# A planned projection stage and a two-engine copy of the attention sums in a transformer block

## The chip, the cores and the metric

The kernel runs on one core of one Trainium2 chip. The metric is the device time of one execution in microseconds (us); the kernel before takes 2050.27 us in the median of three runs (2050.03 to 2050.84). PE is TensorE, DVE is VectorE, ACT is ScalarE, POOL is GpSimd, SP is SyncE, which here only issues DMA transfers.

## The reference

One pre-norm transformer block for 2048 tokens of width 640: 32 heads of 20 channels, and a gated feed-forward part of width 1728. Everything is f32.

```python
def _A_ref(x, wqkv, wo):
    qkv = (lambda x, *d: x.transpose(*d))((x @ wqkv).reshape(B, S, 3, H, Dh), 2, 0, 3, 1, 4)
    q, k, v = qkv[0], qkv[1], qkv[2]
    scores = jnp.einsum("bhqd,bhkd->bhqk", q, k) * (Dh ** -0.5)
    p = _softmax(scores, axis=-1)
    o = jnp.einsum("bhqk,bhkd->bhqd", p, v)
    return (lambda x, *d: x.transpose(*d))(o, 0, 2, 1, 3).reshape(B, S, D) @ wo
def _B_ref(x, w_gate, w_up, w_down):
    return (_silu(x @ w_gate) * (x @ w_up)) @ w_down
h = x + _A_ref(_layernorm(x, axis=-1), A_wqkv, A_wo)
h2 = h + _B_ref(_layernorm(h, axis=-1), B_w_gate, B_w_up, B_w_down)
```

## The kernel before, in words

**Precision.** A factor of a product is split into a rounded part `hi` and a remainder `lo`; ACT writes `hi`, and DVE or POOL subtracts it from the original to make `lo` (function `split`, L88 for `hi`, L89 for `lo`). A product is the sum of three terms, hi·hi, lo·hi and hi·lo.

**Start-up and projections (0 to 338.5 us).** The tokens are four chunks of 512. For each chunk the rows of `x` are loaded, normalized on DVE (statistics L124/L125, then one over the square root by three Newton steps of four small operations each, L98, then the scaling L703), turned round by PE transposes (L735 for the first chunk, L722 for the others, function `flip`), and split into `z_hi` and `z_lo`. The first two blocks of queries and keys run on the whole array (L760). All others are 64-row halves: each `step` of `query_key` or `value` gives PE two products (L547), one for each half of the array, and the two halves run beside each other. While this goes on, PE also computes first scores, whose row maxima the softmax needs later: for those, pairs of products go into one-bank tiles `ps_single` (L186, function `max_differences`, read by ACT L197 and DVE L199; and L210, `max_twice`, read by ACT L222 and DVE L216).

Queries, keys and values travel through DRAM: a finished block goes from PSUM to `e`, `q_stk` or `v_stk` in SBUF, from there to `qk_d` (SP, L305, `emit_store`), and back in the stacked layout that the attention wants (SP, L153, `stack`). SP issues in its program order. The stacked keys of early scores get a difference computed by POOL (L417).

The order of all this is decided when the program is built, by the class `Halves` (an object named `pe`). It keeps a clock for each half of the array and a time at which each engine is free; `pe.use(engine, us)` books work, `pe.sp` books the issue of transfers, `pe.pair` places a pair of score products where the model says that the operands have landed (`there`) and that a bank is free, `pe.flip` places transposes. The list `work` holds 72 items (blocks and value parts); at fixed items it splits weights (`split_w`), loads a chunk, starts a norm (`norm`) and turns the chunk round.

Constants are written by POOL: `k_stk` rows (L142), 14 tiles `mx` with a lowest value (L821), and two tiles `ev` of ones (L895). Three products L826 on `xt` keep PE busy while the first norm runs.

**Attention (338.9 to 1478 us).** 32 units of 16 key tiles. For each key tile PE makes four score products (L1300), ACT the exponential of each (L1306), and PE weighs the values with them (L1310) into one accumulator bank `acc`, of which there is one. In between, three score products per key tile go to `ps_max` (L229, three banks), whose maxima DVE takes (L235). A string for each key tile sets the order on PE: s and S are score products, m and M products for maxima, W the weighing of the key tile two back.

```python
ORDER = ("sMsSmSmW", "SmMsMsSW", "mSmMsSsW")
```

After the last key tile of a unit, `row_sums` copies `acc` to SBUF (L1320, ACT), and four transfers take the sums out of it (L1323).

**After attention (1480 to 2044 us).** Output projection, second norm (`moments` calls its Newton operations in groups), feed-forward part.

Of the kernel before, what the change touches and what calls it, by code (L numbers as in the profile page):

```python
# [47 lines left out]
def tile_block(ctx: ExitStack, tc: tile.TileContext, x, wqkv, wo, wg, wu, wd, out):  # L48
# [42 lines left out]
    def rstd_steps(pool, var, n, tag):  # L91
# [5 lines left out]
        def some(f, *args, **kw):  # L97
# [8 lines left out]
        ]  # L106
        better = [
            some(tt, out=t, in0=r, in1=r, op=ALU.mult),
            some(tt, out=t, in0=t, in1=v, op=ALU.mult),
            some(ts, t, t, -0.5, 1.5, op0=ALU.mult, op1=ALU.add),  # L110
            some(tt, out=r, in0=r, in1=t, op=ALU.mult),
# [189 lines left out]
    def emit():  # L301

        job = stores.pop(0)
        for dst, src, what in job["pieces"]:
            nc.sync.dma_start(dst, src)  # L305
            pe.sp(job["ready"])
            for which, n in what:
                landed[which] += n
                landing[which] = pe.free["sync"] + 3.0
        e_free[job["of"]] = pe.free["sync"] + 3.5  # L310
# [18 lines left out]
    with tc.tile_pool(name="pa", bufs=2) as pa:  # L329
# [10 lines left out]
        def split_sbuf(src, hi, lo, copy):  # L340

            nc.scalar.activation(copy, src, AF.Copy)
            split(copy, hi, lo, nc.gpsimd)
# [6 lines left out]
        def back(now=True):  # L350
            while coming and (not now or coming[0][0] <= pe.now()):
                assert all(landed[1, 0, c] == GD for c in range(NC))
                load_keys(0, coming.pop(0)[1])
                pe.sp(n=4)
# [11 lines left out]
        def place(t):  # L366
# [4 lines left out]
            pe.sp(n=2)  # L371
# [13 lines left out]
        def load_items():  # L385
            for lane, places in lanes:
                while lane:
# [12 lines left out]
                    pe.sp(n=4)  # L400
                    items[lane.pop(0)][3:5] = t, pe.free["sync"]
            for item in items:
                which, _, _, t, at, known, _, base = item
                if not which or t is None or known is not None or pe.now() < at + 4.0:
                    continue
# [10 lines left out]
                for b, a in differences:  # L416
# [3 lines left out]
                    item[5] = pe.use("pool", 1.3) + 0.2  # L420

        def there(n):
# [3 lines left out]
            return t is not None and pe.now() >= at + 4.5  # L426
# [3 lines left out]
        def staged_keys(u, kc, ks, q=None, since=0):  # L430
# [32 lines left out]
            if u == 0:  # L463
                first_unit[0] += len(all_products)
            return [
                (lambda: slot[0] >= since and all(map(there, ns)), lambda a=a: one(*a), a[2])
# [3 lines left out]
        early, others = [], []  # L470
# [37 lines left out]

        class Halves:
# [5 lines left out]
            def __init__(self):  # L515
                self.t = [0.0, 0.0]
                self.free = dict.fromkeys(("vector", "scalar", "pool", "sync"), 0.0)
# [17 lines left out]
            def sp(self, after=0.0, n=1):  # L535
                self.use("sync", 0.4 * n, after)
# [70 lines left out]
            def flip(self):  # L607
# [6 lines left out]
                self.use("pool", 1.3, self.free["scalar"] + 0.1)  # L614
                del self.single[0]

# [80 lines left out]
        def norm(c):  # L697
# [4 lines left out]
            def apply(t):  # L702
# [6 lines left out]
                [(1.1, lambda t=t: stats(pa, xs[c * TPC + t], mv[:, t, :])) for t in range(TPC)]  # L709
                + [(0.2, lambda f=f, g=g: (f(), g())) for f, g in zip(steps[::2], steps[1::2])]  # L710
                + [(0.6, lambda t=t: apply(t)) for t in range(TPC)]
# [7 lines left out]
        def flip(c, k):  # L719
# [6 lines left out]
            pe.flip()  # L726
            copy = chunks[c][:, :, k * P : (k + 1) * P]
            ps, z_hi, z_lo = (a.rearrange("p (t n) -> p t n", t=TPC) for a in (ps, z_hi, z_lo))
            split_sbuf(ps, z_hi, z_lo, copy)
# [37 lines left out]
        def keep(c, m, ps):  # L767
# [7 lines left out]
            else:  # L775
                free = pe.use("scalar", 0.5, start)
                done = pe.use("scalar", 0.5)
                ready = pe.use("pool", 1.3, done + 0.2)
                split_sbuf(ps, e[:, 0], e[:, 1], e[:, 1].bitcast(F32))
# [39 lines left out]
        for u in range(NU):  # L819
            if any(moved(u, kc) for kc in (1, 2)):  # L820
                nc.gpsimd.memset(mxs[u], LEAST)  # L821
        for i in range(4):
            load_w(i)
        warm = ps_one()
        for _ in range(3):
            nc.tensor.matmul(warm, ident, xs[TPC - 1][:, :CH], start=True, stop=True)  # L826
        new_z(0)
        for _, f in norm(0):
# [33 lines left out]
        lns, flips = [], []  # L862
        finish_at = len(work)
        for at, (kind, c, *which) in enumerate(work):
            slot[0] = at
            if at < 9:
                for i in range(split_at[at], split_at[at + 1]):
                    split_w(i + 2)
                    if i % 2 == 1 and loaded < 8:
                        load_w(loaded)  # L870
                        loaded += 1
# [6 lines left out]
            for n in range(1, NC):  # L878
                if at == (2 if n == 1 else begins(n) - 15):
                    lns = norm(n)  # L880
                if n > 1 and at == begins(n) - 16:
                    assert not flips
                    load_x(n)
            if kind == "first":
# [3 lines left out]
            for n in range(1, NC):  # L888
                if at == (7 if n == 1 else begins(n) - 3):
                    assert not lns and all(job["c"] == n - 1 for job in pe.jobs)  # L890
                    new_z(n)
                    flips = [(n, k) for k in range(ND)]
            if at == 6:
                for ev in evs:
                    nc.gpsimd.memset(ev, 1.0)  # L895
                pe.use("pool", 1.5)
# [1116 lines left out]
```

## Time and profile before

| what | us |
|---|---|
| median of 3 runs | 2050.27 (2050.03 to 2050.84) |
| the execution that was profiled | 2046.24 |
| its span in the profile | 2044.5 |
| PE busy in the span | 2012.1 (98%) |
| DVE busy | 1624.6 (79%) |
| ACT busy | 1462.0 (72%) |
| POOL busy | 766.6 (37%) |

The profiled execution is 1.74 us longer than its span and 4.03 us shorter than the median. A line of the profile names the source line, the engine, the operation, the tile written and the tile read; a bracket holds the idle time of the engine just before and what ended it. Matmuls overlap by design: five of them in 1.32 us do not take 0.26 us each, but one step apart plus the end of the last. PEld is the loading of weights into the array.

### The profile page before, as it was taken

How to read it: one execution, taken by the hardware profiler on the slowest of the kernel's cores; microseconds unless marked ns; L12 is line 12 of the kernel's file. 1: busy time of each engine (PE TensorE's matmuls, PEld its weight loads, DVE VectorE, ACT ScalarE, POOL GpSimd, SP SyncE). 2: the span in 40 equal slices, each digit the busy share in tenths (PEclk: the TensorE clock that was granted, in tenths of full speed). 3: DMA queues.
4: the chain of work that ended last, by engine and by line, in shares of the span. 5: the costliest groups of instructions: out<-in, count | busy, mean ns of one | idle time of the engine just before them, and what ended most of it. 6: DMA issues, size and time to landing. Idle time of an engine off the chain costs nothing.

```text
span 2044.5 us, 38964 instructions
## 1 busy us (share of the span) xinstructions
PE 2012.1 (98%) x13656; PEld 1234.4 (60%) x13656; DVE 1624.6 (79%) x3267; ACT 1462.0 (72%) x2937; POOL 766.6 (37%) x1074
## 2 busy tenths in 40 slices
PE   7999999999999999999999999999999999999999
PEld 5888887333333333333333333345598888888888
DVE  7778677888888888888888888886378666676677
ACT  3787888999999999999999999996724222211221
POOL 4443441434343434244431011001145454754555
PEclk9999999999999999999999999999999999999999
DMA  7766554243433443443433013211158654974542
GB/s 230 219 203 222 171 168 146 90 135 117 145 129 107 143 126 128 137 156 127 160 116 118 30 58 86 83 55 61 29 175 301 225 198 157 337 277 157 203 151 93
DMA packets 205123, 305.03 MB, mean 149 GB/s; under 512 B 47664, under 2 KB 82480, under 8 KB 203904
## 3 DMA queue, kind: packets, MB, share of 16 engines
q1 hardware_dynamic: 204832, 302.53, 45.4%
q8 instruction: 109, 1.79, 0.4%
q14 instruction: 86, 0.70, 0.1%
q10 hardware_dynamic: 96, 0.00, 0.0%
HBM read 205.78 MB, written 95.68 MB: 147 GB/s over the span
## 4 chain that ended last, share of the span: by engine, by line
PE 91%; DMA 3%; DVE 2%; POOL 1%; issue 1%; ACT 1%; SPq 0%; POOLq 0%; DVEq 0%; ACTq 0%
PE acc L1310 25%; PE ps_one L1300 16%; PE ps_a L1478 15%; PE ps_max L229 12%; PE ps_b L1572 8%; PE ps_one L547 8%; PE ps_single L210 2%; PE ps_max L1034 2%; PE ps_b L1034 1%; PE ps_single L186 1%; DMA k_stk<-qk_d 1%; DMA units<-w_d 1%; PE ps_one L760 0%; DVE mx L235 0%; PE ps_single L722 0%
## 5 line engine op out<-in xcount | busy, mean ns | idle before, releaser
L1306 ACT ACTIVATE probs<-ps_one 128x512 f32<-128x512 f32 x2048 | 1056.9, 616 | 60.1 <-PE ps_one L1300 23.8
L235 DVE TENSOR_REDUCE mx<-ps_max 128x1 f32<-128x512 f32 x1472 | 925.1, 684 | 117.2 <-PE ps_max L229 72.5
L1300 PE MATMUL ps_one<-q_stk,k_stk 62*128 62x512 f32 x2048 | 582.0, 430 | 0.6 <-ACT ev L807 0.6
L1310 PE MATMUL acc<-probs,v_stk 128*32 128x512 f32 x4096 | 545.2, 604 | 0.0
L229 PE MATMUL ps_max<-k_stk,q_stk 60*128 60x512 f32 x1472 | 488.6, 439 | 1.0 <-DVE mx L235 0.3
L1300 PEld LDWEIGHTS ps_one<-q_stk,k_stk 62*128 62x128 f32 x2048 | 289.4, 184 | 284.8 <-ACT probs L1306 270.8
L229 PEld LDWEIGHTS ps_max<-k_stk,q_stk 60*128 60x128 f32 x1472 | 244.6, 184 | 165.7 <-DVE mx L235 129.0
L1693 DVE TENSOR_TENSOR tmp<-ps_a,tmp 128x512 f32<-128x512 f32 x208 | 141.2, 689 | 120.3 <-PE ps_a L1478 93.5
L1310 PEld LDWEIGHTS acc<-probs,v_stk 128*32 128x32 f32 x4096 | 80.6, 108 | 181.0 <-issue 169.7
L1572 PE MATMUL ps_b<-halves,yp 128*128 128x320 f32 x1032 | 179.3, 308 | 1.7 <-POOL yp L89 1.2
L1572 PEld LDWEIGHTS ps_b<-halves,yp 128*128 128x128 f32 x1032 | 165.1, 188 | 18.2 <-POOL yp L89 1.5
L1478 PE MATMUL ps_a<-t,units 128*128 128x512 f32 x624 | 162.5, 396 | 0.0
L246 POOL CAST both<-neg 128x16 fp32r<-128x16 f32 x32 | 6.6, 206 | 367.7 <-PE ps_one L1300 147.5
L1478 PE MATMUL ps_a<-z,units 128*128 128x512 f32 x516 | 133.8, 394 | 0.0
L89 POOL TENSOR_TENSOR yp<-y,yp 128x256 fp32r<-128x256 f32 x96 | 60.2, 627 | 187.7 <-ACT yp L88 187.7
L1478 PEld LDWEIGHTS ps_a<-t,units 128*128 128x128 f32 x624 | 112.6, 188 | 18.6
L216 DVE CUSTOM_DVE_ANT_0 q_stk<-ps_single,q_stk 128x512 f32<-128x512 f32 x138 | 93.0, 689 | 31.4 <-ACT q_stk L222 25.1
L1577 DVE TENSOR_TENSOR h<-ps_b,h 128x320 f32<-128x320 f32 x248 | 110.0, 481 | 6.8 <-PE ps_b L1572 5.4
L1478 PEld LDWEIGHTS ps_a<-z,units 128*128 128x128 f32 x516 | 93.1, 187 | 15.9
L1345 POOL TENSOR_TENSOR o<-o,rb 128x512 f32<-128x512 f32 x31 | 39.8, 1284 | 159.8 <-DMA rb<-r_d 64.8
L88 ACT ACTIVATE yp<-tmp 128x512 fp32r<-128x512 f32 x40 | 25.3, 633 | 103.1 <-POOL tmp L1565 103.1
L547 PE MATMUL ps_one<-z_hi,w_lo 64*128 64x512 f32 x380 | 98.8, 397 | 0.0
(220 smaller groups left out, 3003.9 us busy)
## 6 DMA issues: line engine op xcount, KB each, us to landing
units<-w_d SPq DMA_DIRECT2D x186, 256.0 KB
w_d<-stage SPq DMA_DIRECT2D x106, 256.0 KB
halves<-j_d SPq DMA_DIRECT2D x70, 320.0 KB
k_stk<-qk_d SPq DMA_DIRECT2D x112, 160.0 KB
j_d<-stage SPq DMA_DIRECT2D x42, 320.0 KB
q_stk<-qk_d SPq DMA_DIRECT2D x64, 160.0 KB
k_stk<-qk_d SPq DMA_DIRECT2D x112, 80.0 KB
rb<-r_d SPq DMA_DIRECT2D x32, 256.0 KB
```

The source lines that it names most:

```text
L216: nc.vector.tensor_tensor_reduce(out=place, in0=pss[1], in1=place, scale=1.0, scalar=LEAST, op0=ALU.add, op1=ALU.max, accum_out=mx[:, b, p ...
L229: nc.tensor.matmul(ps, queries[u][rows, pair, t * P : (t + 1) * P], keys[u // NC][rows, pair, kc * CH : (kc + 1) * CH], start=True, stop=True,
L235: nc.vector.tensor_reduce(mxs[u][:, b, pair, t, kc : kc + 1], ps, axis=AX.X, op=ALU.max)
L547: product = nc.tensor.matmul(job["ps"][:, :out], lhs, rhs, start=(half == 0 and i == 0), stop=(half == 1 and i == job["n"] - 1),)
L1034: nc.tensor.matmul(ps[:, :HALF], a[:, k, :], w[:, k, hs], start=(n == 0), stop=(n == 3 * ND - 1),)
L1300: nc.tensor.matmul(ps, keys[u // NC][rows, p, kt * P : (kt + 1) * P], queries[u][rows, p, :], start=True, stop=True,)
L1306: nc.scalar.activation(probs[p][:, b, :], ps, AF.Exp, scale=scale)
L1310: nc.tensor.matmul(acc[32 * j : 32 * j + 32, :], values[u // NC][:, kt, j * VW : j * VW + 32], probs[j // 2][:, j % 2, :], start=(kt == 0) ...
L1478: nc.tensor.matmul(ps.rearrange("p (t n) -> p t n", t=TPC), w[k][:, i], z[k][:, :, j], start=(first and m == 0), stop=(last and m == len(n ...
L1572: nc.tensor.matmul(ps, a, b, start=(n == 0), stop=(n == len(pairs) - 1))
L1577: nc.vector.tensor_tensor(out=h, in0=ps, in1=h, op=ALU.add)
L1693: add = lambda out, ps, x: nc.vector.tensor_tensor(out=out, in0=ps, in1=x, op=ALU.add)
```

## The change

1. **The planner's model.** `pe.sp` now takes the bytes of a transfer and counts them at 330 KB/us in a clock of their own; it returns the time of landing, and the conditions for placing a pair (`there`, `landing`, the new `queries_at`) use that time in place of fixed allowances. The booking of L417 grows from 1.3 + 0.2 to 1.35 + 1.2, of a pair of Newton operations from 0.2 to 0.4, of a scaling from 0.6 to 1.2. Norm steps wait in the plan for the chunk to land (`x_at`), transposes for the norm (`normed`), and what is left is flushed at `begins(n) + 1`.
2. **Second parts on either engine.** `second_part` puts the subtraction that makes `lo` on DVE (0.75 in the model) when POOL would end over 1.0 later, else on POOL (1.3). Seven subtractions of `z_lo`, `e`, `v_stk` and `z_hi` move to DVE.
3. **Order of the terms** in `query_key`: hi·hi, then z_hi·w_lo, then z_lo·w_hi.
4. **Constants.** The `mx` and `ev` tiles are written by `fill_rest` at item 1 of `work`.
5. **Newton step** in three operations in place of four (12 become 9 for a norm).
6. `row_sums`: ACT copies columns 0 to 255 of `acc` (L1343), DVE columns 256 to 511 (L1344).
7. The products that keep PE busy at the start use a `ps_wide` tile; `moments` takes six Newton operations at a time.

```diff
-            some(tt, out=t, in0=r, in1=r, op=ALU.mult),
-            some(tt, out=t, in0=t, in1=v, op=ALU.mult),
-            some(ts, t, t, -0.5, 1.5, op0=ALU.mult, op1=ALU.add),
-            some(tt, out=r, in0=r, in1=t, op=ALU.mult),
+            some(stt, out=t, in0=r, scalar=-0.5, in1=v, op0=ALU.mult, op1=ALU.mult),
+            some(tt, out=t, in0=t, in1=r, op=ALU.mult),
+            some(stt, out=r, in0=t, scalar=1.5, in1=r, op0=ALU.add, op1=ALU.mult),
...
-            def sp(self, after=0.0, n=1):
-                self.use("sync", 0.4 * n, after)
+            def sp(self, after=0.0, n=1, kb=0):
+                end = self.use("sync", 0.4 * n, after)
+                begin = max(self.free["dma"], end - 0.4 * n + 0.5)
+                self.free["dma"] = begin + kb / 330
+                self.free["sync"] = max(end, self.free["dma"] - 5.0)
+                return max(self.free["sync"] + 2.0, self.free["dma"] + 1.3)
...
-            return t is not None and pe.now() >= at + 4.5
+            return t is not None and pe.now() >= at + 0.3
...
+            def second_part(self, after):
+                ends = [max(self.free[e], after, self.now()) + us for e, us in SECOND]
+                if ends[1] + 1.0 < ends[0] and self.free["vector"] < after + 0.5:
+                    return nc.vector, self.use("vector", SECOND[1][1], after)
+                return nc.gpsimd, self.use("pool", SECOND[0][1], after)
...
-            terms = ((z_hi, w_hi), (z_lo, w_hi), (z_hi, w_lo))
+            terms = ((z_hi, w_hi), (z_hi, w_lo), (z_lo, w_hi))
...
-        for u in range(NU):
-            if any(moved(u, kc) for kc in (1, 2)):
-                nc.gpsimd.memset(mxs[u], LEAST)
+
+        def fill_rest():
+            for ev in evs:
+                nc.gpsimd.memset(ev, 1.0)
+            for u in range(NU):
+                if any(moved(u, kc) for kc in (1, 2)):
+                    nc.gpsimd.memset(mxs[u], LEAST)
+            pe.use("pool", 3.5)
...
+                if at == n == 1:
+                    fill_rest()
...
-        nc.scalar.activation(o, acc, AF.Copy)
+        nc.scalar.activation(o[:, : CH // 2], acc[:, : CH // 2], AF.Copy)
+        nc.vector.tensor_copy(o[:, CH // 2 :], acc[:, CH // 2 :])
```

What it does to the order on the engines, at three places. The first is POOL in the first 35 us, with the change (w_lo is the lower part of a slice of the weights; the tiles' numbers are the buffers').

```order
L142 MEMSET k_stk_115 32x4096 x2
L89 TENSOR_TENSOR w_lo<-raw,w_hi 128x5x128 x2
L837 MEMSET ev_155 128x768
L837 MEMSET ev_156 128x768
L840 MEMSET mx_120 128x64
L840 MEMSET mx_121 128x64
L840 MEMSET mx_122 128x64
```

Eleven more `mx` tiles follow, and then three more `w_lo`. Before, the 14 `mx` tiles stood ahead of the first `w_lo`, and the two `ev` tiles behind the fifth; now all 16 stand between the second and the third `w_lo`.

The second place is SP's queue where the first pair of score products gets its queries, before (-) against after (+ and unmarked); `qk_d` is the DRAM buffer, `k_stk` and `q_stk` are stacked keys and queries.

```order
 L305 DMA qk_d<-q_stk 80x2x512
 L305 DMA qk_d<-q_stk 16x2x512
+L153 DMA k_stk_115<-qk_d 40x2x512
+L153 DMA k_stk_115<-qk_d 20x2x512
+L153 DMA k_stk_115<-qk_d 40x2x512
+L153 DMA k_stk_115<-qk_d 20x2x512
 L153 DMA q_stk<-qk_d 40x2x512
 L153 DMA q_stk<-qk_d 20x2x512
```

Four loads of keys now stand ahead of the four loads of those queries; before, they came behind them.

The third place is DVE at the end of an attention unit, with the change and with the semaphores that each instruction waits for (L235 takes a maximum, L1355 is the reciprocal of the sums, L242 ends a unit's maxima).

```order
L235 TENSOR_REDUCE mx_125<-ps_max 128x1 [waits PE_49] x6
L1344 COPY o<-acc 128x256 [waits DMAHW5_49,DMAHW4_49,DMAHW6_49,DMAHW3_49,Activation_49]
L235 TENSOR_REDUCE mx_125<-ps_max 128x1 [waits PE_49] x9
L1355 RECIPROCAL r<-r 128x16 [waits DMAHW3_49,DMAHW2_49,DMAHW4_49,DMAHW1_49,DMAHW0_49]
L235 TENSOR_REDUCE mx_125<-ps_max 128x1 [waits PE_49] x17
```

The copy L1344 is new among the maxima, and it waits for ACT's semaphore: the value it waits for is the one that ACT's own copy L1343 of the same unit sets. On PE the number of products and, from the attention on, their order are the same in both programs.

More of the change, by code (lines that the diff above doesn't have):

```diff
@@ L465, in staged_keys @@
             return [
-                (lambda: slot[0] >= since and all(map(there, ns)), lambda a=a: one(*a), a[2])
+                (
+                    lambda: slot[0] >= since and all(map(there, ns))
+                    and (q is not None or pe.now() >= queries_at.get(u, math.inf)),
+                    lambda a=a: one(*a), a[2],
+                )
                 for a in all_products
             ]
-        early, others = [], []
+        early, others, queries_at = [], [], {}
         def third_unit():
@@ L777, in keep @@
                 done = pe.use("scalar", 0.5)
[L778 to L779 removed]
+                engine, ready = pe.second_part(done + 0.2)
+                split_sbuf(ps, e[:, 0], e[:, 1], e[:, 1].bitcast(F32), engine)
             r0 = m // 2 * P
```

69 lines of the change are left out of this document (35 added, 34 removed).

## The prediction

> **What bounds the kernel now.** I read first the table of stretches, cut where PE's idle time or clock changes (columns: length, busy us of PE, PEld, DVE, ACT, POOL, granted clock, DMA share, GB/s).
>
> ```profile
> 26.40:46.00 19.60, 17.77 (x133) 14.96 (x132) 17.80 (x39) 8.36 (x13) 10.28 (x8) 1.00 0.66 207
> 46.00:48.00 2.00, 0.80 (x4) 0.54 (x6) 1.91 (x3) 0.38 (x1) 1.22 (x1) 1.00 0.61 166
> 48.00:52.00 4.00, 4.00 (x24) 3.77 (x22) 1.81 (x7) 1.77 (x5) 0.00 (x0) 0.57 0.82 245
> 52.00:100.00 48.00, 46.92 (x423) 41.37 (x421) 35.09 (x172) 38.00 (x104) 21.04 (x16) 1.00 0.72 219
> 100.00:220.00 120.00, 116.81 (x1076) 105.19 (x1073) 97.44 (x334) 97.35 (x202) 48.97 (x38) 1.00 0.66 209
> 236.00:239.00 3.00, 0.69 (x8) 0.37 (x6) 1.40 (x4) 0.82 (x2) 2.58 (x3) 1.00 0.59 203
> 239.00:243.00 4.00, 4.00 (x29) 3.85 (x27) 1.60 (x5) 1.79 (x3) 0.00 (x0) 0.57 0.00 0
> 243.00:338.50 95.50, 93.61 (x925) 87.77 (x923) 73.96 (x253) 78.34 (x162) 33.41 (x30) 1.00 0.60 180
> 338.50:2044.50 1706.00, 1696.36 (x10863) 952.29 (x10863) 1368.37 (x2390) 1212.85 (x2411) 627.93 (x949) 1.00 0.42 139
> ```
>
> PE bounds every stage. In the projections (26.4 to 338.5) it is wholly idle for 1.83 + 1.20 + 1.08 + 3.19 + 2.31 + 1.89 = 11.5 us in these rows. Twice, behind a hole in PE of over 2 us, four microseconds run at a clock of 0.57; each costs 4 × 0.43 = 1.7 us. Third, one half of the array can wait while the other works, and then PE still counts as busy. To size that I laid the half products one behind the other, each half by itself, in the order of the program, at the step that these rows give:
>
> ```profile
> 27.66 1.32 PE L547 MATMUL ps_one<-z_lo,w_hi 64*128 64x512 f32 x5
> 335.20 0.89 PE L547 MATMUL ps_one<-w_hi,z_lo 64*128 64x320 f32 x5
> ```
>
> About 0.39 or 0.31 us of a row is the last product's own length, so four steps take 0.93 and 0.58: 0.231 and 0.145 us each. Without any wait the stage would take 284.6 us by that, an estimate; it took 311.9, from 26.4 to 338.3. Of the 27.3 us of stalls some 11.5 are idle PE, 3.4 the low clock, and 12 half an array waiting. What the idle PE waited for, over the first 340 us:
>
> ```profile
> PE ps_single L186 <- DVE mx L199: 2.9, 4, 1.5
> PE ps_one L547 <- POOL z_lo L89: 2.3, 1, 2.3
> PE ps_single L186 <- DMA k_stk<-qk_d: 1.8, 1, 1.8
> PE ps_single L186 <- POOL raw L417: 1.6, 1, 1.6
> PE ps_single L186 <- DMA q_stk<-qk_d: 0.9, 1, 0.9
> PE ps_single L210 <- POOL raw L417: 0.9, 1, 0.9
> ```
>
> So the changed planner can win at most some 27 us here, and the attention has to be looked at for itself.
>
> **Start-up: -1.0 (0 to -1.4).**
>
> ```profile
> 7.65 4.39 PE L826 MATMUL ps_one<-xt,ident 128*128 128x512 f32 x6 [7.65 <-DMA xt<-in_A_x]
> 8.48 1.27 POOL L821 MEMSET mx<- 128x64 f32 x14
> 8.82 0.95 DVE L98 TENSOR_SCALAR v_a<-mv 128x4 f32<-128x4 f32 x1
> 10.01 0.16 DVE L98 TENSOR_TENSOR t_a<-r_a 128x4 f32<-128x4 f32 x1
> 10.21 0.16 DVE L98 TENSOR_TENSOR t_a<-t_a,v_a 128x4 f32<-128x4 f32 x1
> 13.07 1.86 PE L735 MATMUL ps_wide<-ident,xt 128*128 128x128 f32 x15 [1.03 <-DVE xt L703]
> 90.22 0.17 DVE L98 TENSOR_SCALAR v_a<-mv 128x4 f32<-128x4 f32 x1
> ```
>
> The first DVE operation of the norm takes 0.95 beside POOL's 14 memsets and 0.17 at 90 us: 0.78 come free when the memsets go. Three Newton operations at a pitch of 0.20 are 0.60 more. But the transposes waited only 1.03 for DVE; behind that PE's own warming products end (12.04). So 1.0 of 1.38.
>
> **First pair of scores: -0.5 (-4.4 to +1.5).** The pair at 46.29 waits 1.8 for keys and 0.9 for queries, and the low clock adds 1.7.
>
> ```profile
> 31.94 3.01 SPq L305 DMA_DIRECT2D qk_d<-e  x4
> 36.62 1.63 SPq L153 DMA_DIRECT2D k_stk<-qk_d  x4
> 42.00 1.58 SPq L153 DMA_DIRECT2D q_stk<-qk_d  x4
> 43.44 1.41 POOL L895 MEMSET ev<- 128x768 f32 x2
> ```
>
> The plan asks for it 31 half products later (163 instead of 132), 31 × 0.231 / 2 = 3.6 us. But four key loads now stand ahead of the query loads on SP (1.63, and 480 KB at the 207 GB/s of that stretch are 2.3), and the memsets, 1.27 + 1.41 = 2.7 us of POOL, stand ahead of the third w_lo; the weight load that waits for that w_lo's buffer has the stores of L305 queued behind it on SP. Start-up takes 1.0 of the 2.7 back. That makes 1.6 to 2.3 and about 1.5, 3.1 to 3.8 later, against 3.6 later asked: about the same wait as before.
>
> **Pacing round the norm: -2 (-3.7 to +1).** The four waits of L186 for DVE (2.9) stand at 96 to 110 us, where the norm's operations come between the maxima in DVE's order; by the order-only sum 3.7 us are lost there. Booked at 0.4 and 1.2 in place of 0.2 and 0.6 the pairs come later, and the norm is three operations shorter. I take about half, for the plan is still a plan.
>
> **z_lo: -4.0 (-4.0 to 0).**
>
> ```profile
> 234.84 2.52 POOL L417 TENSOR_TENSOR k_stk<-k_stk,raw 128x512 fp32r<-128x512 f32 x2 [0.32 <-DMA k_stk<-qk_d]
> 237.31 1.26 POOL L89 TENSOR_TENSOR z_lo<-xt,z_hi 128x512 fp32r<-128x512 f32 x1
> 238.63 0.49 PE L547 MATMUL ps_one<-z_lo,w_hi 64*128 64x512 f32 x1 [2.31 <-POOL z_lo L89]
> ```
>
> The last z_lo of the chunk sat on POOL behind two differences of 1.26 each. With w_lo as the second term it is asked for five products, 1.15 us, later; the transposes start a step earlier where the plan allows, and DVE may take a z_lo. 2.31 and the 1.7 of low clock behind it go. Already with a hole of 1.2 left the clock should hold, for the trace has a hole of 1.47 us at 106.18 with a clock of 1.00 in its stretch.
>
> [...]
>
> **Waits for L417: -1.5 (-2.5 to 0).** 1.6 + 0.9; the difference is now booked as ready 1.05 later, which covers one wait and most of the other. **Other half-array waits: -3 (-6 to +2).** A quarter of the 12 us; the view does not name them. **The order itself: +3.4 (0 to +3.4).** The same sum over the new order gives 288.0 for 284.6, all of it in the last blocks, where score products that were put off run with one half empty. **New waits: +1 (0 to +3).** Seven subtractions come to DVE, each about as long as a maximum (1.89 / 3 = 0.63 in a row below) and mostly in its idle time, and POOL's memsets a w_lo.
>
> **The copy of the sums: +2.3 (-4.8 to +11).** One unit's boundary:
>
> ```profile
> 513.12 0.16 PEld L1310 LDWEIGHTS acc<-probs,v_stk 128*32 128x32 f32 x8 [0.37 <-issue]
> 514.45 0.63 ACT L1320 ACTIVATE o<-acc 128x512 f32<-128x512 f32 x1
> 514.69 1.89 DVE L235 TENSOR_REDUCE mx<-ps_max 128x1 f32<-128x512 f32 x3 [0.24 <-PE ps_max L229]
> 515.24 0.16 PEld L1310 LDWEIGHTS acc<-probs,v_stk 128*32 128x32 f32 x8 [0.36 <-ACT o L1320]
> 517.09 0.18 PEld L1300 LDWEIGHTS ps_one<-q_stk,k_stk 62*128 62x128 f32 x1 [0.17 <-ACT probs L1306]
> 517.52 0.16 PEld L1310 LDWEIGHTS acc<-probs,v_stk 128*32 128x32 f32 x8 [0.25 <-issue]
> PEld acc L1310 <- ACT o L1320: 10.6, 29, 0.4
> 88.89 0.37 DVE L199 CUSTOM_DVE_ANT_0 v_stk<-ps_single,v_stk 128x256 f32<-128x256 f32 x1
> 333.09 1.34 ACT L197 ACTIVATE q_stk<-ps_single 128x256 f32<-128x256 f32 x4 [0.46 <-PE ps_single L186]
> ```
>
> From weighing to weighing PE takes 2.12 us (515.24 - 513.12), and 2.28 behind the boundary (517.52 - 515.24), because ACT is 0.63 late and a score product waits 0.17 for it. The nearest rows for the halves: ACT takes 0.33 apiece on 256 columns (1.34 / 4, first one 0.38), DVE 0.37 to 0.42. So ACT is 0.3 earlier and that 0.16 goes. But the order shows that DVE's copy waits for ACT's. It runs at 0.41 to 0.83 behind the start of ACT's copy. `acc` is free at 0.88 for 0.63 now, just behind the weighing's due time (515.24 - 514.45 = 0.79); and the next maximum starts at 0.75 for 0.24 now, so the three banks of `ps_max` come free 0.51 later, less the 0.24 that DVE idles each period. Put through the three kinds of boundary that the three order strings give, the second weighing stands at 3.23, 3.01 and 3.23 for 3.08 (517.52 - 514.45 = 3.07): +0.08 on average, times the 29 boundaries at which weighing waits for the copy (the row of the waits), +2.3. Were the copies side by side, ACT's relief alone would stay: -0.10 to -0.16 a unit, -3 to -4.8.
>
> [...]
>
> **Rest: -0.3 (-1 to +1).** Later norms' Newton steps, and one step's shift of the transposes behind the attention, under a PE that waits little there (9.6 us in 1706).
>
> **Sum.** -1.0 - 0.5 - 2 - 4 - 1.5 - 3 + 3.4 + 1 + 2.3 - 0.3 = -5.6. Against the profiled execution: 2046.24 - 5.6 = 2040.6; it lies 4.03 under the median, so 2044.7.
>
> **Rivals.** *R1, the plan fits.* Pair -4.4, norm -3.7, L417 -2.5, others -6 and nothing new: -1.4 - 4.4 - 3.7 - 4 - 2.5 - 6 + 3.4 + 2.3 - 0.3 = -16.6, 2033.7. For it: bytes are now counted. Against: DMA moved 166 to 245 GB/s in the rows above, and the plan counts 330.
>
> *R2, slower: DVE's copy holds the third bank of the maxima.* If that bank governs at every boundary, the full 0.51 - 0.16 = 0.35 to 0.37 is paid 29 times, +10.7 for +2.3, and the time is 2053.1. It decides if DVE's copy ends later than 0.95 behind the start of ACT's. Against it: DVE's slack of 0.24 a period and the shorter ACT copy; for it: three cross-engine steps that I had to place by neighbours. With a copy as long as a full maximum (0.69) it would be 2061.
>
> *R3, stalls that only move.* SP stays in order and the data come slower than booked: pair, norm, L417 and others give nothing. -5.6 + 7.0 = +1.4, 2051.7. For it: the four key loads ahead of the queries. Against: the term order and the longer bookings need no DMA.
>
> *R4, the copies do overlap* (the wait is over before DVE comes to it): -4 for +2.3, 2038.4.
>
> **How the numbers follow.** Chances: forecast 0.36, R1 0.12, R2 0.20, R3 0.24, R4 0.08. The range leaves out most of R1 below and R2's far end above: 2035 to 2056. About 0.2% (4.1 us) is what a measurement of this kernel tells from no change. Under 2046.2 lie two thirds of the forecast, R1, R4 and a little of R3: 0.47. Over 2054.4: half of R2, a sixth of R3, a little of the forecast: 0.18. The rest, 0.35, lies between.
>
> **What would show it.** Start-up: the first transposes at 12.0 with no wait for DVE. First pair: its wait for `q_stk`, and a clock of 0.57 or not. z_lo: no L547 wait for POOL over 1 us, no dip near 240. Norm: the wait of L186 for DVE under 1. Copy: the period behind each boundary 2.3 or more, and a wait of L229 for DVE there; a unit 0.08 longer. The prediction is wrong if a unit grows by over 0.3 us, or if the projections, 311.9 long, end more than 12 us earlier or no earlier at all.

## The result, and the profile after

The changed kernel takes 2053.51 us in the median (2051.44 to 2055.87, 10 runs), the kernel before 2050.2 (2046.2 to 2056.07, 10 runs): 1.001 times the time before, 95% interval 1.0001 to 1.002. It is slower by some 3 us where 5.6 us less were forecast. The time lies inside the stated range, on the other side of no change.

The profiled execution after takes 2053.59 us, span 2051.8. Against the profile of before its first attention score comes at 338.3 (338.9 before), its last weighing at 1486.6 (1479.1 before), and from there both need the same 565.2 to 565.4 us to the last instruction. So the projections, with the start-up, won 0.6 us where 7.6 were forecast, and the attention lost 8 where 2.3 were.

Four views show it. First the longest waits of PE over the first 340 us, without those of the start-up (line, what ended the wait, us in all, times, longest).

```profile
PE ps_single L186 <- DMA q_stk<-qk_d: 3.4, 2, 3.1
PE ps_one L1323 <- DVE mx L199: 1.4, 1, 1.4
PE ps_single L210 <- DMA xt<-in_A_x: 1.2, 1, 1.2
PE ps_single L186 <- ACT q_stk L88: 1.0, 1, 1.0
PE ps_single L210 <- DVE mx L216: 0.8, 2, 0.7
PE ps_single L186 <- DMA raw<-qk_d: 0.8, 1, 0.8
```

The waits that the forecast wanted away are away: none of L186 for the maxima of DVE before the end of the stage, none of the half products for z_lo, none for POOL's differences. Others stand in their place. The stretches after, cut at the holes:

```profile
46.00:49.20 3.20, 0.07 (x2) 0.07 (x1) 0.69 (x1) 0.60 (x1) 1.01 (x1) 0.92 0.58 190
49.20:56.00 6.80, 6.55 (x26) 4.41 (x28) 2.83 (x9) 3.55 (x8) 1.53 (x2) 0.53 0.70 213
67.00:69.40 2.40, 0.54 (x5) 0.28 (x3) 0.79 (x6) 1.19 (x3) 2.40 (x3) 0.96 0.84 259
69.40:76.00 6.60, 6.60 (x35) 5.76 (x36) 1.99 (x10) 2.82 (x7) 1.68 (x2) 0.50 0.62 194
336.90:338.30 1.40, 0.00 (x0) 0.00 (x0) 1.25 (x8) 0.83 (x3) 0.00 (x0) 1.00 0.22 86
338.30:346.00 7.70, 7.68 (x31) 3.62 (x33) 5.56 (x9) 6.09 (x12) 0.00 (x0) 0.56 0.41 125
```

Three holes, 3.1, 1.9 and 1.4 us, and behind each a low clock of 6.83 us, twice as long as the spells of before (3.41). From the first half product on that is some 6.5 us lost to the clock ahead of the first score, for 3.4 before. The third hole is PE waiting at the end of the stage for DVE to take the maxima of the score products that the new order put there; a low clock follows and falls into the first attention unit, so that the second unit begins at 379.1 for 378.1, although the first score came 0.6 earlier: 1.5 us.

The start-up, for comparison with the rows of before; the last row here is of before, the counterpart of the one above it:

```profile
7.28 4.75 PE L847 MATMUL ps_wide<-xt,ident 128*128 128x512 f32 x6 [7.28 <-DMA xt<-in_A_x]
8.33 0.17 DVE L98 TENSOR_SCALAR v_a<-mv 128x4 f32<-128x4 f32 x1
10.51 2.18 DVE L718 TENSOR_SCALAR xt<-xt,mv,r_a 128x640 f32<-128x640 f32 x4
11.86 1.80 PE L750 MATMUL ps_wide<-ident,xt 128*128 128x128 f32 x15
16.64 2.57 PE L775 MATMUL ps_one<-z_hi,w_hi 128*128 128x512 f32 x10 [1.65 <-DVE z_lo L89]
17.91 4.02 PE L760 MATMUL ps_one<-z_hi,w_hi 128*128 128x512 f32 x10 [1.65 <-DVE z_lo L89]
```

The transposes start behind the warming products without waiting for DVE, and the first block at 16.64 for 17.91. Of these 1.27 us 0.37 are the tokens landing earlier (7.28 for 7.65); 0.9 belong to the change. The ten products themselves take 2.57 for 4.02: in the profile of before a spell of half clock (17.66 to 21.07 us) falls on them, and after has none there. So the half products begin at 23.67 for 26.40, and 1.5 of these 2.7 us are not the change's: of four profiles with the projections of before (before and runs 2, 3, 4) two have that spell and two have not. From the first half product to the first score PE then takes 314.7 us, 2.2 more than before (312.5).

Then one boundary of the attention, the one between the fifth and the sixth unit as in the prediction, and the row of all waits for the copy:

```profile
517.33 0.42 ACT L1343 ACTIVATE o<-acc 128x256 f32<-128x256 f32 x1
517.78 0.42 DVE L1344 COPY o<-acc 128x256 f32<-128x256 f32 x1 [0.45 <-ACT o L1343]
518.12 3.67 DVE L235 TENSOR_REDUCE mx<-ps_max 128x1 f32<-128x512 f32 x6
518.26 0.16 PEld L1333 LDWEIGHTS acc<-probs,v_stk 128*32 128x32 f32 x8 [0.50 <-DVE o L1344]
520.05 0.18 PEld L229 LDWEIGHTS ps_max<-k_stk,q_stk 60*128 60x128 f32 x1 [0.41 <-DVE mx L235]
520.72 0.16 PEld L1333 LDWEIGHTS acc<-probs,v_stk 128*32 128x32 f32 x8 [0.37 <-issue]
PEld acc L1333 <- DVE o L1344: 15.0, 29, 0.6
```

DVE stands 0.45 us before its copy, for ACT's. The next unit's weighing starts 0.93 behind the start of ACT's copy (518.26 - 517.33; 0.79 before), and the one after it another 2.46 later (2.28 before): DVE takes six maxima without a pause, and the third score product for a maximum waits 0.41 for its bank. Over 28 units the last period of a unit is 2.272 in the mean (2.124 before) and the first 2.377 (2.289 before): 0.236 a boundary, 6.6 us.

### The profile page after: what moved, and what is told of

The parts are those of the page before. It is cut to its first block, busy times and chain, and to the rows that moved or that the text cites. A ratio compares the mean times of both kernels' runs of the same rounds, so it can differ in the third digit from the quotient of the medians.

```text
span 2051.8 us, 39039 instructions
## 1 busy us (share of the span) xinstructions
PE 2018.7 (98%) x13656; PEld 1238.6 (60%) x13656; DVE 1627.8 (79%) x3285; ACT 1460.7 (71%) x2936; POOL 755.8 (37%) x1067
## 5 line engine op out<-in xcount | busy, mean ns | idle before, releaser
L235 DVE TENSOR_REDUCE mx<-ps_max 128x1 f32<-128x512 f32 x1472 | 922.0, 684 | 100.7 <-PE ps_max L229 58.5
L229 PE MATMUL ps_max<-k_stk,q_stk 60*128 60x512 f32 x1472 | 495.3, 441 | 1.8 <-DVE mx L235 0.2
L556 PE MATMUL ps_one<-z_lo,w_hi 64*128 64x512 f32 x380 | 99.1, 397 | 0.0
```

The lines of the kernel that those rows point to most:

```text
L229: nc.tensor.matmul(ps, queries[u][rows, pair, t * P : (t + 1) * P], keys[u // NC][rows, pair, kc * CH : (kc + 1) * CH], start=True, stop=True,
L235: nc.vector.tensor_reduce(mxs[u][:, b, pair, t, kc : kc + 1], ps, axis=AX.X, op=ALU.max)
L556: product = nc.tensor.matmul(job["ps"][:, :out], lhs, rhs, start=(half == 0 and i == 0), stop=(half == 1 and i == job["n"] - 1),)
```

## The experiments

Theory A: the copy in two halves costs about 0.24 us at each boundary because DVE's half waits for ACT's; the projections' gain is eaten by holes at which data come later than planned, with a long low clock behind each. Rivals: the attention is slower because of the state in which the projections leave it; the copy costs because DVE is the scarce engine, whatever is copied; the holes would open in any order. The runs of before spread from 2042.9 to 2059.5 us, so medians over 5 to 12 runs carry about 1 to 2 us each, and traces have to say the rest. The runs were made in four groups, each with its own runs of before (medians 2049.66 for runs 1 to 4, 2048.99 for 5 to 8, 2049.23 for 9 to 12, 2047.82 for 13 and 14), and a ratio is to these. The runs of before in the result had 2050.2; a difference between kernels of two groups is uncertain by as much as these medians differ.

**1. one_copy**, the changed kernel with the copy undone:

```diff
-        nc.scalar.activation(o[:, : CH // 2], acc[:, : CH // 2], AF.Copy)
-        nc.vector.tensor_copy(o[:, CH // 2 :], acc[:, CH // 2 :])
+        nc.scalar.activation(o, acc, AF.Copy)
```

> The changed kernel with its copy of the sums put back: ACT copies all 512 columns, DVE none; everything else of the change stays. Theory A (the two-engine copy costs about 0.24 us at each of 29 boundaries, 2.46 + 2.26 us for the two periods around it against 2.29 + 2.12 before): 7 us below the changed kernel, so about 2046.5 and 3 to 4 us below the kernel before, a unit of the attention back at 34.28. Theory B (the attention is slower because of where the projections leave it, its low clock at the start, and not because of the copy): no more than 1 us below the changed kernel, units stay at 34.5.

2049.85 us, ratio 0.9996 (0.9982 to 1.001). The two periods at a boundary are back at 2.121 and 2.295. The median falls only 3.7 below the changed kernel where 7 were expected (3.1, each against its own runs of before). This profile holds something else, in the eleventh unit, which may be a part of that:

```profile
694.06 0.16 PEld L1333 LDWEIGHTS acc<-probs,v_stk 128*32 128x32 f32 x8 [0.36 <-issue]
...
695.74 0.25 DVE L1354 RECIPROCAL r<-r 128x16 f32<-128x16 f32 x1 [2.51 <-DMA r<-o]
695.91 3.61 DVE L235 TENSOR_REDUCE mx<-ps_max 128x1 f32<-128x512 f32 x6
698.93 0.20 PEld L1333 LDWEIGHTS acc<-probs,v_stk 128*32 128x32 f32 x8 [0.65 <-issue]
```

DVE waits in its order for a transfer of the sums (2.51 us), PE runs out of banks (its product for a maximum waits 1.05 us for DVE), and two weighings stand 4.9 us apart (698.93 and 694.06). Run 8 takes that up.

**2. two_copies**, the reverse edit alone on the kernel before.

> The kernel before with the copy in two halves alone (ACT 256 columns, then DVE 256). Theory A: 7 us slower than before, about 2057, with periods of 2.26 and 2.46 (2.29 and 2.22 at every third boundary) around a boundary. Theory B: within 1 us of before.

2057.18 us, ratio 1.0039 (1.0025 to 1.0052). Its periods at a boundary are 2.276 and 2.375, those of the changed kernel. The copy by itself costs 0.24 us a boundary, whatever the projections do. The rival that their state slows the attention is out.

**3. dve_busy**, ACT's copy whole and a useless operation on DVE:

```diff
         nc.scalar.activation(o, acc, AF.Copy)
+        nc.vector.tensor_tensor(out=busy[:, 1], in0=busy[:, 0], in1=busy[:, 0], op=ALU.mult)
```

> The kernel before, ACT's copy whole, and a useless DVE operation of 256 columns (SBUF to SBUF, on a tile of its own, some 0.3 us, no wait) at the place of the second copy; its result is used by nothing. It occupies DVE without holding the accumulator bank and without waiting for ACT. If the loss comes from DVE being occupied as such (later maxima): +0.08 to +0.17 a boundary, +2 to +5 us. If it comes from the wait behind ACT's copy (DVE stands still till 0.45 and the bank is held till 0.87): under +1 us, since the maxima have 0.24 us of slack a period.

2050.47 us, ratio 1.0005 (0.9993 to 1.0017); periods 2.122 and 2.302, 0.01 more than before. The operation takes 0.46 us, and at this place, where it waits for nobody, it costs nothing that shows.

**4. dve_only**, one copy, by DVE:

```diff
-        nc.scalar.activation(o, acc, AF.Copy)
+        nc.vector.tensor_copy(o, acc)
```

> The kernel before, with DVE copying all 512 columns and ACT none. No copy waits for another copy, and ACT's 0.63 us go. If two copies in series are what costs, this one is free at about 0.65 behind the end of the weighing, the score products no longer wait for ACT, and the time is within 2 us of before (-3 to +2). If DVE is the scarcer engine at the boundary, whatever is copied, its 0.63 to 0.69 us push the third bank of the maxima as far as the two halves do: +3 to +7 us.

2048.1 us, ratio 0.9995 (0.998 to 1.001). The same boundary, and the row of the waits:

```profile
518.90 0.68 DVE L1320 COPY o<-acc 128x512 f32<-128x512 f32 x1
519.50 3.67 DVE L235 TENSOR_REDUCE mx<-ps_max 128x1 f32<-128x512 f32 x6
519.75 0.16 PEld L1310 LDWEIGHTS acc<-probs,v_stk 128*32 128x32 f32 x8 [0.37 <-DVE o L1320]
522.09 0.16 PEld L1310 LDWEIGHTS acc<-probs,v_stk 128*32 128x32 f32 x8 [0.36 <-issue]
PEld acc L1310 <- DVE o L1320: 10.7, 29, 0.5
```

DVE's six maxima follow without a pause as in the changed kernel, yet the weighings wait 10.7 us in all for 15.0, and the periods are 2.126 and 2.243, 0.04 less than before in sum. So it is not the load on DVE: two copies in series hold the bank and DVE longer (0.87 from the start of the first to the end of the second) than one copy of everything by either engine (0.63 or 0.68). Whether the bank or DVE's lost time carries more of the 0.24 no run parts.

In the changed kernel DVE stands 0.45 us before its half, for ACT's (517.78 us in the profile after). No run let the two halves overlap, so what they would take side by side is not shown.

**5. pair_later**, one_copy with the first queries booked 4 us later:

```diff
-                    queries_at[u] = pe.sp(n=4, kb=750) + 0.3
+                    queries_at[u] = pe.sp(n=4, kb=750) + (4.3 if u == 0 else 0.3)
```

> The changed kernel with ACT's single copy, and the first pair's queries booked as landing 4 us later in the plan, so that the pair stands 19 half products (2.1 us) further back. Theory A (the hole of 2.7 to 3.1 us at 49 us comes from the four key loads ahead of the query loads on SP, and the 6.8 us of half clock behind it hang on the hole): hole under 1 us, no low clock at 49, first weighing of the attention 3 to 6 us earlier than the 343.8 of the single-copy kernel, median 3 to 5 us lower. Theory B (the stage waits for data in any case; a hole taken away opens later): first weighing within 1.5 us of 343.8.

2054.13 us, ratio 1.0025 (1.0015 to 1.0036). The hole moved to 53 us and stayed at 3.07, now for POOL, and the whole order behind it changed; near the end stands

```profile
330.44 0.63 PE L556 MATMUL ps_one<-w_hi,z_hi 64*128 64x320 f32 x1 [5.93 <-ACT ev L822]
```

This run does not tell the theories apart: one number in the plan moves every later decision.

**6. terms_old**, one_copy with the old order of the three terms, and **12. joined_terms**, the same edit on the joined kernel of run 11:

```diff
-            terms = ((z_hi, w_hi), (z_hi, w_lo), (z_lo, w_hi))
+            terms = ((z_hi, w_hi), (z_lo, w_hi), (z_hi, w_lo))
```

> The changed kernel with ACT's single copy and the old order of the three terms (z_lo second, w_lo last). If the order of the terms is what took the z_lo wait away (2.3 to 3.4 us of hole near 240 and the low clock behind it in the profiles of the old order): a z_lo wait of POOL of 1 us or more comes back, and 2 to 5 us. If it was the transposes' earlier start and the planner's bookings: no such wait, within 1.5 us of the single-copy kernel.

> The same as the joined kernel, with the old order of the three terms. Against it this measures the order of the terms a second time: 3 us below it if the single run's gain was real (then the new order costs time), within 1 us of it if the order does not matter, 2 us above it if a wait for z_lo comes back.

2046.82 us (0.9987, 0.9978 to 0.9996) against 2049.85, and 2043.29 (0.9965, 0.995 to 0.998) against 2043.86. The 3 us of the first (2.4, each against its own runs of before) did not come again. No wait of the half products for z_lo stands in either profile's list, so it is not the order of the terms that took it away. What is left is the planner's bookings and the second parts that moved to DVE, which no run parts.

**7. constants_first**, one_copy with all 16 constant tiles at the start (`fill_rest()` ahead of the first `load_w`).

> The changed kernel with ACT's single copy and all 16 constant tiles written at the start again, ahead of the first chunk's weights on POOL. Forecast of the record: start-up 0.8 us longer (the first norm operation at 0.95 in place of 0.17), but 2.7 us of POOL gone ahead of the third w_lo, so the queries of the first pair land earlier: total within 1 us. Rival: memsets of 2.7 us at the start delay w_hi/w_lo of the first blocks as well: 2 to 3 us slower.

2044.74 us, ratio 0.9977 (0.9965 to 0.9989), 5.1 below one_copy (4.4, each against its own runs of before), where within 1 was expected. The start-up is longer as forecast (the first two small operations of the norm take 0.74 and 1.18 for 0.17 each, and the first half product comes 1.2 later behind PE's first product), but the first pair waits less:

```profile
48.91 0.46 PE L186 MATMUL ps_single<-k_stk,q_stk 60*128 60x512 f32 x1 [1.26 <-POOL k_stk L416]
49.89 0.47 PE L186 MATMUL ps_single<-k_stk,q_stk 60*128 60x512 f32 x1 [0.51 <-DMA raw<-k_stk]
```

1.77 us of hole for 2.66 in one_copy, and low clocks of 3.41 us where one_copy has 6.83. The first score comes at 335.2 for 338.4. The edit also drops the 3.5 us that the plan booked on POOL, but the order of the products on PE is the same in both traces, as far as their records go.

**9. constants_late**, the kernel before with only the constants moved to item 1.

> The kernel before, with only its 16 constant tiles moved to where the change writes them (POOL, item 1, ahead of the third w_lo); Newton, planner and copy as before. Theory A (2.7 us of POOL there hold the weight load, the stores and so the first pair's data): the hole at 46 us longer by 1 to 2.5 us, the start-up 0.8 to 1 us shorter, 1 to 5 us slower than before. Theory B (the move is worth its start-up gain, and the middle of the projections does not care): 1 us faster than before.

2052.03 us, ratio 1.0009 (0.9997 to 1.0021), 2.8 above its runs of before. POOL, and the hole:

```profile
28.60 1.42 POOL L883 MEMSET ev<- 128x768 f32 x2
29.96 1.27 POOL L886 MEMSET mx<- 128x64 f32 x14
31.19 1.56 POOL L89 TENSOR_TENSOR w_lo<-raw,w_hi 128x640 fp32r<-128x640 f32 x1
```

```profile
47.88 0.47 PE L186 MATMUL ps_single<-k_stk,q_stk 60*128 60x512 f32 x1 [3.95 <-DMA q_stk<-qk_d]
49.03 0.76 PE L186 MATMUL ps_single<-k_stk,q_stk 60*128 60x512 f32 x1 [0.68 <-DMA q_stk<-qk_d]
```

4.6 us of hole for 2.7 to 3.1 in the four profiles with the constants in their old place, with a start-up 0.9 shorter. The interval still takes in no change; theory A's longer hole stands in this one trace.

**10. constants_6**, one_copy with the constants behind POOL's first difference:

```diff
-                if at == n == 1:
+                if at == 6 and n == 1:
                     fill_rest()
```

> The changed kernel with ACT's single copy, the 16 constant tiles at item 6 (where the kernel before wrote the two tiles of ones) in place of item 1, behind the first difference of keys on POOL. Theory A: the start-up gain stays (first norm operation 0.17) and the third w_lo is not held: 4 to 6 us faster than the single-copy kernel, about 2044 and at or below the kernel with the constants first. Rival: any 2.7 us of POOL in the projections cost what they cost at item 1: no faster than the single-copy kernel.

2046.06 us, ratio 0.9985 (0.9973 to 0.9997). The hole of the first pair is 1.8 and draws no low clock, and the start-up keeps its gain; but the hole near 68 is 4.5 us in this profile, with 6.83 of low clock. Better than item 1 by 3.8 (3.4, each against its own runs of before), not better than the start: in this profile the first pair's part of the theory holds, the forecast number does not.

**8. recip_later**, one_copy with the reciprocal one key tile later:

```diff
-            if kt == (3 if sooner else 4) and tail:
+            if kt == (3 if sooner else 5) and tail:
```

> The changed kernel with ACT's single copy, and the reciprocal of the sums (a DVE instruction that waits for the transfer of the sums) one key tile later in every unit but the last two. The single-copy kernel's profile has three long periods (4.9, 3.9, 2.9 us) at 694 to 703 us, where DVE stood 2.5 us before the reciprocal, and a low clock behind them; its runs fall in two groups, 2044.7 to 2047.0 and 2049.3 to 2051.1. If the late transfer is the cause: no period over 2.6 us in the attention, the upper group goes, median 2045 to 2047. If not: median within 1 us of 2049.9, two groups as before.

2047.82 us, ratio 0.9991 (0.9983 to 1.0). No period over 2.6 us is left between the first weighing and 1370 us (the last units have longer ones in every profile). All 8 other profiles in which ACT alone copies have a pause of this kind in the third or the eleventh unit, with a longest period of 2.6 to 4.9 us (before 3.63, at 693). But the runs of recip_later still spread from 2044.2 to 2049.9, and its median lies above the 2045 to 2047 expected, so the pause was not what parts them. The pause is shown; its cure rests on one profile, and its share in the median is not shown.

**11. joined**: constants first, DVE alone copies, reciprocal later.

> The changed kernel with the constants first, the sums copied by DVE alone, and the reciprocal one key tile later: the three edits that were neutral or better by themselves. If they add up: 2044.7 - 1.5 - 2 = 2041 to 2043. If the reciprocal's pauses and the copy are worth nothing beside the constants: 2044 to 2046.

2043.86 us, ratio 0.9972 (0.9959 to 0.9984): faster than both kernels, by 0.3% against before, and between the two expectations. Its projections are those of run 7, but its profile has 3.1 us of hole at the first pair, where run 7's has 1.77, and its first score comes at 339.1 for 335.2. So run 7's short hole is one profile's and not the edit's alone; what both profiles have is one window of half clock (3.41 us) behind the hole near 49 us and one near 70, for two (6.83 us) at each place in one_copy.

**13. land_2** and **14. rate_280**, each one number of the plan on the joined kernel:

```diff
-                    items[lane.pop(0)][3:5] = t, pe.sp(n=4, kb=750) + 0.3
+                    items[lane.pop(0)][3:5] = t, pe.sp(n=4, kb=750) + 2.3
```

```diff
-                self.free["dma"] = begin + kb / 330
+                self.free["dma"] = begin + kb / 280
```

> The joined kernel, with every staged load of the early scores booked as landing 2 us later in the plan. Laid out without waits its order takes 289.7 us for 288.0 (an estimate). Theory A (the holes near 49 and 68 us are loads that land after the plan thought, and each draws 3.4 to 6.8 us of half clock): the hole near 68 under 1 us, 3 to 6 us won there against 1.7 given to the order, median 2040 to 2043. Theory B (what is put off is paid back in the tail and new holes open elsewhere): 2043 to 2047, no gain over the joined kernel.

> The joined kernel, with 280 KB/us in the planner in place of 330 (the trace moves 183 to 259 GB/s in the stretches of the projections). Order without waits: 290.9 for 288.0. Theory A (the rate is what the plan has wrong): holes near 49 and 68 shorter, 2 to 4 us won after paying 2.9 for the order: 2040 to 2042. Theory B: the rate only moves products into the tail, 1 to 4 us slower than the joined kernel, 2045 to 2048.

land_2: 2045.82 us, ratio 0.9988 (0.9978 to 0.9997), no gain over the joined kernel. The hole near 68 is gone and one of 1.96 near 48 is left; the order's 1.7 and 13.65 us of low clock at the end of the stage take some of that back. Even so its second attention unit begins at 378.3 for 380.4 in joined; its profile loses 2.5 us behind the attention, where PE waits 1.8 for POOL (1.2 in joined) and a low clock of 3.41 us at 1790 follows, which no other profile has. rate_280: 2040.4 us (5 runs), ratio 0.9965 (0.9952 to 0.9977), the lowest time of all. Its stretches:

```profile
46.00:80.00 34.00, 33.09 (x290) 28.57 (x290) 22.09 (x110) 28.82 (x78) 14.90 (x12) 1.00 0.72 225
320.00:333.40 13.40, 11.66 (x66) 8.52 (x62) 9.92 (x46) 9.63 (x25) 0.00 (x0) 0.86 0.29 94
333.40:346.00 12.60, 12.60 (x59) 5.95 (x59) 8.75 (x14) 9.46 (x19) 0.00 (x0) 0.61 0.14 40
```

From 46 to 80 us there is 0.9 us of idle PE and no low clock, and the attention's first score comes at 333.4 for 339.1 in the joined kernel, although its order alone is 2.9 us longer by the estimate above; the 13.65 us of low clock at the end of the stage are there too. So holes near 49 and 68 are not forced: they go when transfers are booked to land later, by rate_280 at both places and by land_2 at the second. That the rate itself is what the plan has wrong is not shown, for one number moves all later decisions (run 5). Its interval overlaps that of the joined kernel (0.9959 to 0.9984), and in the medians, each against its own runs of before, it is 2 us ahead; that it beats the joined kernel is likely and not shown.

## Why the prediction was wrong, point by point

- **The copy, +2.3: the mechanism was right, the size was not.** It measured +6.6 in the trace and +7.5 in run 2. The step that failed is the placing of the second weighing at 3.23, 3.01 and 3.23 behind ACT's copy. Three boundaries of the trace have 3.15, 3.39 and 3.39. At the slower kind the score product that waits for its bank starts at 2.72 (520.05 - 517.33), and another one and the weighing follow at 0.33 each, to 3.39; my sum gave less to these two, and did not carry on that the first weighing itself was 0.14 to 0.18 late (0.93 for 0.75 to 0.79). R2 named this bank and asked 0.35 a boundary; 0.24 were paid, with DVE's copy ending at 0.87, below the 0.95 that I had put as the point of decision. So the rule by which I chose between the forecast and R2 was wrong too.
- **First pair, -0.5: wrong.** 3.1 us of hole for 2.7, and 6.83 of half clock for 3.41: +2.1. I had put the delays at 3.1 to 3.8 against 3.6 and so called it even, and let the clock cost 1.7 in either case. The second step failed more than the first: the hole is 2.7, 3.1, 2.7 and 3.0 in the four profiles with the old projections and 3.1, 2.7 and 3.8 in the three with the new (after, runs 1 and 8), while the spell behind it is 3.41 in all four and 6.83 in all three. The medians of runs 7 and 9 say that the place of the constants matters (4.4 less than run 1, 2.8 more than before); that POOL's 2.7 us ahead of the third w_lo do it by the length of this hole is borne out by runs 7 and 9 and not by run 11.
- **Start-up, -1.0: right.** 0.9 to the first block; and from PE's first product to the first half product the two old profiles without a spell of half clock there take 17.4 us, the three new ones 16.2 to 16.5. The move of the constants, which is a part of it, loses more further on: 4.4 to 5.1 us between run 7 and run 1. Costed apart, the two halves of one edit looked even.
- **Norm -2, L417 -1.5: right**, both waits gone whole in this profile, 2.9 and 2.5 us (run 1 has 1.1 of the second left). **z_lo -4.0: the gain right, the first reason wrong**: hole and low clock near 240 are away, and stay away with the old term order. The other reasons that the prediction gave, the transposes' start and a z_lo on DVE, stay possible.
- **Other half-array waits, -3: right.** By the same sum: 338.3 - 23.7 = 314.6 us, 288.0 without waits, 10.6 idle, 6.5 low clock, and 9.5 of half an array waiting, for 12; the 9.5 is a remainder, from one profile.
- **Order, +3.4: at its place**, in the last blocks, and there it brought the hole of 1.4 (0.6 before). The low clock at the attention's start, some 1.5 us, which no term had, is not the new order's alone: runs 2, 3 and 4, in the old order, have 6.83 us of it there too.
- **New waits, +1: too small.** The hole near 68 us is 1.9 us of idle PE and 3.3 of low clock, and 1.2, 0.7 and 0.7 stand at 164, 180 and 301. R3 had these. Runs 13 and 14, which book transfers as landing later, do without the hole near 68.
- **The sum's base.** I set the terms against one profile. In four profiles whose projections are those of before (before, and runs 2, 3, 4) the first score comes at 338.9, 345.7, 340.6 and 341.0: the shown one is the best of them. The three with the changed projections (after, runs 1 and 8) have 338.3, 338.4 and 341.0. The means are 341.6 and 339.2: 2.3 us won, not 0.6, and 2.1 at the start of the second unit (382.2 and 380.1), so that the low clock at the attention's start is no loss of its own. 2.1 won against 6.6 lost is 4.5 slower, for 3.3 in the medians; that sum is an estimate from single profiles. Of the 7.6 us forecast for the projections some 2 came.

What stays open: what the attention's pause for the sums is worth in the median, by which path the place of the constants works, and why run 10 had the longer hole near 68.

## What to carry to other kernels

Splitting a copy between two engines won nothing here, where both halves read one bank: look in the order for the semaphore of the one on the other, and cost the two in series, with the bank and the second engine held for the sum (0.87 us here, for 0.63 or 0.68 of one copy). Where PE is nearly always busy, price a wait by the hole and the low clock behind it, which was the larger of the two near 68 us of after (3.3 us for 1.9), and follow a moved instruction to everything queued behind it before calling a move even. Where the stalls of a stage differ from run to run, take the base of a sum from several profiles.

## What the runs showed of the hardware

The low clock came in spells of 3.41 us or a multiple of it: three of 3.413 us in the clock records of before, three of 6.827 in those of after, each at a granted clock of 0.50. Counted from the first clock record, at 10.83 us in before and 11.17 in after, they start at whole multiples of 3.413 us. The spells that end inside the kernel do so in all 16 profiles, and last one to four of these steps, here called windows; some by their start in multiples:

```
before    2 (x1)   11 (x1)   67 (x1)
after    11 (x2)   17 (x2)   96 (x2)
joined   11 (x1)   17 (x1)   96 (x2)
rate_280 93 (x4)
```

The length of a spell does not follow from the hole ahead of it: behind 3.13 us stand two windows (after), behind 1.9 us in all also two (67 to 76 us, after), behind 3.38 one (dve_only, at 240 us), behind 1.05 + 0.76 none (constants_6). Cut at the marks of this grid, the profiles show how busy PE was in each window; two windows each of after and of joined, at the first pair:

```profile
45.31:48.72 3.41, 0.72 (x5) 0.25 (x2) 0.69 (x1) 0.60 (x1) 0.53 (x1) 1.00 0.56 185
48.72:52.14 3.42, 2.73 (x8) 1.53 (x9) 1.16 (x5) 1.43 (x4) 0.73 (x1) 0.50 0.66 207
48.16:51.58 3.42, 0.68 (x3) 0.42 (x5) 1.13 (x3) 0.68 (x2) 1.26 (x1) 1.00 0.53 171
51.58:54.99 3.41, 3.41 (x15) 2.16 (x15) 1.21 (x6) 2.05 (x5) 0.00 (x0) 0.50 0.81 222
```

Both holes are 3.1 us. That of after ends at 49.13, behind the mark at 48.72, so that PE is idle for 0.69 of the low window too, and a second low window follows. That of joined ends at 51.35, ahead of the mark at 51.58; PE fills the low window, and the clock behind it is 1.00. Between 22 and 300 us the 16 profiles count as follows. The 30 spells there begin behind windows in which PE was 0.14 to 0.56 busy (0.35 and 0.32 in before, 0.21 and 0.50 in after), and none behind a busier one (between 0.49 and 0.56 the clock stayed at 1.00 at times, as behind the 0.54 at 273.66 us of before). A spell went on behind the 14 low windows in which PE stood idle at some time (0.64 to 0.998 busy; 0.80 and 0.96 in after), and ended behind 29 that PE filled (four of them in before and after) and one that it did not (0.90, constants_late). A hole of 1.8 us in all had one low window behind it where it lay in one that was 0.48 busy (constants_first), and none where it was split between two that were 0.75 and 0.72 busy (constants_6). At half of a spell's length, an estimate, the clock cost 1.7 or 0 us behind these two holes of 1.8, and 3.4 or 1.7 behind the two of 3.1 (after, joined). The first clock record, from which the grid counts, comes at 10.8 us in before and at 14.9 in dve_busy, whose projections are the same; that this makes runs of one kernel differ by several us is my guess, and not shown. At the attention's start the reading fails: spells begin there behind windows in which PE was 0.56 to 1.00 busy (0.58 in after), and go on behind full ones (1.00 in after); what draws them stays open.
